# Moving a convolution kernel's input transform of the second sequence in among the first unit's products, with copies of 1008 columns

## The chip, the cores and the metric

The kernel runs on one core of one Trainium2 chip. The core's engines run side by side, each through its own queue in order: TensorE (PE in the profile, with its weight loads as PEld), VectorE (DVE), ScalarE (ACT), GpSimd (POOL) and SyncE (SP), which here only issues transfers. PE writes its results to PSUM, eight banks of 512 float32 columns for each of 128 partitions; DVE and ACT read them from there. The metric is the device time of one execution in microseconds (us), lower is better.

## What is computed

```
B, S, C = 2, 2048, 1024          # x: (B, S, C), w: (3, C, C), bfloat16
xp = pad(x, one row of zeros at both ends of S)
y = sum(einsum('bsc,cd->bsd', xp[:, k:k + S, :], w[k]) for k in range(3))
y = (y - mean) * (g / sqrt(var + 1e-5)) + b
return silu(y)
```

It is a convolution of width 3 along the sequence, over two sequences of 2048 rows with 1024 channels in and out, then a normalisation by channel and SiLU.

## The kernel before

The convolution is done in a transformed domain (Winograd's method, six output rows from eight points): each sequence is cut into NB = 342 blocks of R = 6 rows, NJ = 8 transformed values j stand for each block and channel, and for each j there is one matrix product over the channels. The stages are:

- **Input transform.** The rows of a sequence are loaded in NW = 17 row blocks ("windows") of 128 rows, 21 transform blocks each (the last one, the "short block", has 33 rows and 6). For each window and each tile of 128 channels one matmul (L265) multiplies the window by a fixed matrix `rm`, 128 x 168 columns (8 values j times 21 blocks; 48 columns in the short block). A **transform job** is a group of such matmuls into a pair of PSUM banks, followed by one copy to the tile `T_sb` in SBUF, by ACT (L276) or DVE (L278); the builder chooses the engine by a running clock of its own (`ends`, `busy`, `cost`). `T_sb` is one tile of [128, 8 channel tiles, 8 j, 684 blocks]; sequence 1 has the columns 0 to 341 of its last axis, sequence 2 the columns 342 to 683. Before the change a job is one window and four channel tiles, four matmuls and a copy of 672 columns, and a sequence has 33 jobs.
- **Weight transform.** The three weight matrices of 128 output channels become six (`u0`, `u1`, `u2`, two each) by sums on POOL (L174, L184, L194) with some scaling on ACT (L162, L180) and DVE. For the first 128 channels `prepare_first(0)` issues it, behind the job with number `W0_USE`.
- **Units.** A unit (`Unit.run`) is 128 output channels of one sequence: eight products in the order j = 1, 3, 2, 4, 5, 6, then 0 and 7 (which run behind product 5 and 6 of the following unit, `prev.rest`). A product is eight matmuls of 342 columns (L311), one for each channel tile, which accumulate in one PSUM bank. Copies by ACT (L322, L324) and sums by DVE (L329) combine them, ACT applies SiLU (L334), and the result goes out by transposing transfers (L443) and stores (L456). There are 16 units; unit 0 is sequence 1, unit 1 sequence 2 with the same weights. Unit 0 uses banks 0 to 3.

The order on every engine is that in which the builder emits the instructions (`manual_schedule`); the tile framework adds a semaphore wait wherever an instruction touches a region of a tile that an earlier instruction on another engine wrote or read. `ahead` emits jobs one after another, with the bank pairs 0, 2, 4, 6 in turn. The last `AMONG` = 18 jobs of sequence 2 are emitted by the object `between`, which `product` calls after each matmul: up to product 5 of unit 0, in the bank pairs 4, 6, 1 in turn.

The loads stand on SP's queue in this order: windows 1 to 16 and then window 0 of sequence 1, with the three weight loads of the first 128 channels behind the fifth, seventh and ninth; then the same windows of sequence 2, with the weights of the next 128 channels behind the sixth, ninth and twelfth. Window 0 has a tile of its own (`xfirst`, with a zero row, loaded in two parts of 112 and 15 rows, L124 and L125); the others share twelve buffers (`xpool`), so that a load waits for the jobs of the window twelve loads earlier. When unit 0 has been emitted, `xpool` is closed and the next weights (L146) use its space.

Of the kernel before, what the change touches and what calls it, by code (L numbers as in the profile page):

```python
# [11 lines left out]
BF16 = mybir.dt.bfloat16  # L12
# [3 lines left out]
P = 128  # L16
R = 6
NJ = 8
W0_AT = (4, 6, 8)
W0_USE = 18  # L20
W1_AT = (5, 8, 11)
AMONG = 18
XBUFS = 12
WT = 21

@with_exitstack
def kernel(
# [10 lines left out]
    nc = tc.nc  # L38
    B, S, C = x.shape
# [63 lines left out]
    rm = transform_matrix()  # L103

    clock = {"pe": 3500.0, "act": 0.0, "dve": 0.0, "dma": 2600.0}
    cost = {"act": (0.833, 190.0), "dve": (1.042, 150.0)}
    bank_free = {}

    def ends(e, size):
        return max(clock[e], clock["pe"] + 100.0) + cost[e][0] * size + cost[e][1]  # L110

    def busy(e, size):
        clock[e] = ends(e, size)

    order = list(range(1, NW)) + [0]
    xwin = {}
    xfirst = consts.tile([P, C], BF16, name="xfirst")
    nc.gpsimd.memset(xfirst[0:1, :], 0.0)

    def load_x(bi, wi):  # L120
        if wi == 0:
            xw = xfirst
            cut = (P - 1) // 16 * 16
            nc.sync.dma_start(out=xw[1:1 + cut, :], in_=x[bi, 0:cut, :])  # L124
            nc.sync.dma_start(out=xw[1 + cut:P, :], in_=x[bi, cut:P - 1, :])  # L125
        else:
            xw = xpool.tile([P, C], BF16, name="xw")
            lo = R * WT * wi - 1
            hi = min(lo + P, S)
            nc.sync.dma_start(out=xw[0:hi - lo, :], in_=x[bi, lo:hi, :])  # L130
        clock["dma"] += 730.0
        xwin[bi, wi] = xw, clock["dma"]

    w_all = w.rearrange("k (ct p) d -> p k ct d", p=P)
# [4 lines left out]
    def load_w(pair, k, half=None):  # L139

        if (pair, "tile") not in raw:
            raw[pair, "tile"] = wpools[pair % 2].tile([P, 3, CT, 2, P], BF16, name=f"wch{pair % 2}")
        wch = raw[pair, "tile"]
        h0, h1 = (0, 2) if half is None else (half, half + 1)
        cols = slice((2 * pair + h0) * P, (2 * pair + h1) * P)
        nc.sync.dma_start(  # L146
            out=wch[:, k, :, h0:h1].rearrange("p c h d -> p c (h d)"), in_=w_all[:, k, :, cols]
        )
        clock["dma"] += 1200.0 * (h1 - h0)
        for h in range(2):  # L150
            raw[2 * pair + h] = wch[:, :, :, h]
# [74 lines left out]
    ident = consts.tile([P, P], BF16, name="ident")  # L226
    make_identity(nc, ident)

    def params():

        v = ps[:, 7].bitcast(BF16)[:, 0:4 * DC]
        nc.tensor.transpose(v, rows, ident[0:4 * DC, 0:4 * DC])
        nc.scalar.copy(prm, v.rearrange("p (q dc) -> p q dc", q=4))
# [12 lines left out]

    def t_jobs(bi):

        for wi in order:
            n = LAST if wi == NW - 1 else WT  # L250
            rows = min(P, S - (R * WT * wi - 1))
            n0 = bi * NB + wi * WT
            nb = 1 if CT * NJ * n <= 512 else 2
            nct = CT if nb == 1 else CT // 2
            for c0 in range(0, CT, nct):
                yield xwin[bi, wi], rows, n, n0, c0, nct, nb

    def t_job(job, bank):
        (xw, there), rows, n, n0, c0, nct, nb = job
        clock["pe"] = max(clock["pe"], there, bank_free.get(bank, 0.0))  # L260
        size = nct * NJ * n
        src = ps[:, bank:bank + nb, 0:size // nb]
        v = src.rearrange("p b (c j n) -> p b c j n", j=NJ, n=n)
        for c in range(nct):
            nc.tensor.matmul(  # L265
                v[:, c * nb // nct, c % (nct // nb)], lhsT=xw[0:rows, (c0 + c) * P:(c0 + c + 1) * P],
                rhs=rm[0:rows, :, 0:n], start=True, stop=True,
            )
        dst = T_sb[:, c0:c0 + nct, :, n0:n0 + n].rearrange("p (b c) j n -> p b (c j) n", b=nb)
        src = src.rearrange("p b (q n) -> p b q n", n=n)  # L270
        clock["pe"] += nct * NJ * n / 2.3
        e = min(("act", "dve"), key=lambda k: ends(k, size))
        busy(e, size)
        bank_free[bank] = clock[e] + 100.0
        if e == "act":
            nc.scalar.copy(dst, src)  # L276
        else:
            nc.vector.tensor_copy(dst, src)  # L278
# [8 lines left out]
    class Unit:  # L287
# [64 lines left out]
        def rest(self, between, last=5, first=6):  # L352


            return [
                (min(last, 5), self.silu_inner), (last, lambda: self.last(between)),
                (first, lambda: self.first(between)),
            ]

        def run(self, between, also=(), prepare=None):  # L360

            def behind(n):
                for at, f in also:
                    if at == n:
                        f()

            b0, b1, b2, b3 = self.bank
            sl = slice(self.lo, self.hi)  # L370
            sd = dpool.tile([P, 2, NB], FP32, name="sd")[:, :, sl]
            t0 = dpool.tile([P, 2, NB], FP32, name="t0")[:, :, sl]
            t2 = dpool.tile([P, 2, NB], FP32, name="t2")[:, :, sl]
            self.y23 = t1 = ypool2.tile([P, 2, NB], FP32, name="t1")[:, :, sl]
            self.product(3, 1, False, between)
            pa = self.copy(3)
            behind(1)
            self.product(0, 3, False, between)
            pb = self.copy(0, by=4.0)
            behind(2)  # L380
            self.product(3, 2, True, between)
            self.copy(3, dst=sd[:, 0])
            self.combine(sd[:, 1], pa, 2.0, b3, ALU.subtract)
            behind(3)
            self.product(0, 4, True, between)
            behind(4)
            self.combine(b1, b0, -2.0, pb)
            for t, a in ((t0, -0.0125), (t1, -0.05), (t2, -0.2)):
                self.combine(t, self.low, a, sd)
            idle(dve_work)  # L390
            if prepare:
                prepare_w(prepare)
            self.product(2, 5, False, between)
            pc = self.copy(2)
            if not prev:
                for _ in range(4):
                    between()
            behind(5)
            self.product(2, 6, True, between)
            self.combine(b3, b2, -0.5, pc)  # L400
            self.combine(self.low, self.high, -1.6, t0)
            self.combine(t1, self.high, -0.4, t1)
            self.combine(self.high, self.high, -0.1, t2)
            behind(6)
            if prepare:
                idle(act_work)
                idle(dve_work)
# [61 lines left out]
    def ahead(jobs, job_n):  # L469
        for job in jobs:  # L470
            t_job(job, job_n % 4 * 2)
            if job_n == 0:
                params()
            if job_n == 4:
                scales()
            if job_n == W0_USE:
                prepare_first(0)
            job_n += 1

    jobs0 = list(t_jobs(0))  # L480
    ahead(jobs0, 0)
    for i, wi in enumerate(order):
        load_x(1, wi)
        if i in W1_AT:
            load_w(0, W1_AT.index(i), 1)
    jobs1 = list(t_jobs(1))
    ahead(jobs1[:-AMONG], len(jobs0))

    class Between:

        n = done = 0
        jobs = jobs1[-AMONG:]

        def __call__(self):
            self.n += 1
            while self.jobs and self.done * 46 < self.n * AMONG:
                t_job(self.jobs.pop(0), (4, 6, 1)[self.done % (3 if self.n <= 4 * CT else 2)])
                self.done += 1

    between = Between()  # L500
    seq = [(dc, bi) for dc in range(DC) for bi in range(B)]
# [1 line left out]
    for i, (dc, bi) in enumerate(seq[:-1]):  # L503
        unit = Unit(dc, bi, i % 2 * 4)
        unit.run(
            between, prev.rest(between, *((4, 5) if i >= len(seq) - 3 else (5, 6))) if prev else (),
            1 if i == 0 else 2 if i == 2 else dc + 2 if bi == 1 and 0 < dc < DC - 2 else None,
        )
        if i == 0:
            while between.jobs:  # L510
                between()
            xwin_scope.close()
            olast = ctx.enter_context(tc.tile_pool(name="olast", bufs=3))
            wpools[1] = ctx.enter_context(tc.tile_pool(name="wpool1", bufs=1))
        if i in (0, 4, 8):
            for k in range(3):
                load_w(i // 4 + 1, k)
        if i == len(seq) - 2:
            prev.turn(olast, ((1, R), (0, 1)))
        elif prev:  # L520
            prev.turn()
        if before:
            before.store()
        before, prev = prev, unit
# [49 lines left out]
```

## Time and profile before

| | us |
|---|---|
| median of 3 runs (lowest, highest) | 191.89 (191.7, 192.23) |
| the profiled execution | 191.58 |
| its span, first to last instruction | 189.8 |
| busy in it: PE, DVE, ACT, POOL | 177.1, 157.0, 111.3, 136.8 |
| first transform matmul | 3.89 |
| first matmul of a product | 27.04 |
| the last window of sequence 1 (`xfirst`) is there, its jobs start | 20.02 |

The span is counted from the first instruction; outside it lie 191.58 - 189.8 = 1.78 us. "Busy" of PE is from the start of a matmul to its modelled end, and matmuls overlap, so that the distance of starts says more than the busy time. In a line of the timeline stand the start, the time, engine, line, operation, written tile <- read tiles, shapes, the number of instructions, and in brackets how long the engine was idle before and what ended that. The granted clock of TensorE is 0.993 of full over the span.

### The profile page before, as it was taken

The numbers are of one execution on the slowest core, as the hardware profiler recorded it, in microseconds if no ns is written. First come the engines' busy times: TensorE is split into PE (matmuls) and PEld (weight loads), VectorE is DVE, ScalarE is ACT, GpSimd is POOL, SyncE is SP. The second block draws the span as 40 slices with busy tenths as digits, with TensorE's granted clock in tenths as the row PEclk, the third lists the DMA queues.
The fourth block names the chain that finished last, engine by engine and source line by source line (L and its number), as shares of the span: only waits on it lengthen the run. The fifth ranks groups of instructions, "written<-read, shape, count | busy, mean of one in ns | idle before, by whom it ended". The sixth has DMA issues, their size and how long they took to land.

```text
span 189.8 us, 3717 instructions
## 1 busy us (share of the span) xinstructions
PE 177.1 (93%) x1397; PEld 126.3 (67%) x1397; DVE 157.0 (83%) x222; ACT 111.3 (59%) x187; POOL 136.8 (72%) x76
## 2 busy tenths in 40 slices
PE   1978989999999999999999999999999999999990
PEld 1966758666666666666666666666666666669980
DVE  5588976689978799998799989889988996769680
ACT  3688876783547474546445654655455556454790
POOL 5559999905798869999999999889999972000000
PEclk9999999999999999999999999999999999999997
DMA  5999999075060929398659494997495696867544
GB/s 180 325 329 301 343 335 301 23 203 134 6 118 20 195 54 206 95 268 204 115 129 161 108 200 137 226 209 134 108 208 115 144 109 129 173 136 161 133 99 108
DMA packets 86832, 31.71 MB, mean 167 GB/s; under 512 B 73438, under 2 KB 82654, under 8 KB 86814
## 3 DMA queue, kind: packets, MB, share of 16 engines
q1 hardware_dynamic: 85775, 31.23, 71.8%
q10 hardware_dynamic: 1039, 0.25, 0.6%
q8 instruction: 11, 0.18, 0.4%
q14 instruction: 7, 0.06, 0.1%
HBM read 14.82 MB, written 8.39 MB: 122 GB/s over the span
## 4 chain that ended last, share of the span: by engine, by line
PE 81%; DMA 10%; ACT 3%; SPq 2%; issue 1%; DVE 1%
PE ps L311 77%; DMA xw<-in_x_dram 7%; PE ps L265 4%; DMA xfirst<-in_x_dram 3%; ACT yT L334 2%; SPq L130 2%; SPq L146 1%; PE ps L419 1%; DVE T_sb L278 0%; ACT T_sb L276 0%; ACT o L420 0%; DVE o L420 0%; ACT pc L322 0%
## 5 line engine op out<-in xcount | busy, mean ns | idle before, releaser
L311 PE MATMUL ps<-T_sb,u 128*128 128x342 bf16 (+2 forms) x816 | 120.0, 299 | 0.3
L311 PEld LDWEIGHTS <-u 128*128 128x128 bf16 x816 | 76.8, 97 | 33.6 <-issue 0.5
L194 POOL TENSOR_TENSOR u<-e,w1x 128x1024 bf16<-128x1024 f32 x32 | 70.3, 2222 | 12.3 <-DVE e L176 12.1
L311 PE MATMUL ps<-T_sb,wch 128*128 128x342 bf16 (+2 forms) x272 | 42.5, 299 | 0.0
L334 ACT ACTIVATE yT<-ps,beta,scale 128x342 bf16<-128x342 f32 (+5 forms) x51 | 34.1, 704 | 11.8 <-PE ps L311 11.8
L329 DVE SCALAR_TENSOR_TENSOR t<-ps,sd 128x684 f32<-128x684 f32 (+2 forms) x51 | 39.1, 821 | 0.6
L194 POOL TENSOR_TENSOR u<-e,wch 128x1024 bf16<-128x1024 f32 x16 | 37.6, 2370 | 1.0 <-DMA wch<-in_w_dram 0.4
L311 PEld LDWEIGHTS <-wch 128*128 128x128 bf16 x272 | 25.7, 97 | 11.5
L322 ACT COPY pc<-ps 128x342 f32<-128x342 f32 (+2 forms) x34 | 14.5, 427 | 31.9 <-PE ps L311 29.4
L265 PE MATMUL ps<-rm,xw 128*128 128x168 bf16 (+1 forms) x256 | 25.8, 247 | 6.8 <-DVE rm L100 3.9
L276 ACT CAST T_sb<-ps 128x672 bf16<-128x672 f32 (+1 forms) x37 | 25.5, 737 | 7.9 <-PE ps L265 7.8
L278 DVE CAST T_sb<-ps 128x672 bf16<-128x672 f32 x29 | 23.7, 855 | 7.4 <-PE ps L265 7.0
L265 PEld LDWEIGHTS <-xw 128*128 128x128 bf16 (+1 forms) x256 | 21.1, 104 | 11.5 <-DMA xw<-in_x_dram 5.7
L329 DVE SCALAR_TENSOR_TENSOR ps<-ps,t 128x684 f32<-128x684 f32 (+2 forms) x34 | 28.3, 831 | 0.6
L176 DVE SCALAR_TENSOR_TENSOR e<-wch 128x1024 f32<-128x1024 bf16 x14 | 27.1, 1937 | 0.0
L329 DVE SCALAR_TENSOR_TENSOR ps<-ps,pc 128x342 f32<-128x342 f32 (+2 forms) x34 | 16.9, 498 | 8.9 <-PE ps L311 7.0
L174 POOL TENSOR_TENSOR e<-wch 128x1024 f32<-128x1024 bf16 x8 | 19.0, 2372 | 3.9 <-DMA wch<-in_w_dram 3.9
L334 ACT ACTIVATE yT<-t,beta,scale 128x684 bf16<-128x684 f32 (+2 forms) x17 | 15.7, 925 | 0.0
L329 DVE SCALAR_TENSOR_TENSOR sd<-pc,ps 128x342 f32<-128x342 f32 (+2 forms) x17 | 8.3, 487 | 8.4 <-ACT sd L322 8.3
L329 DVE SCALAR_TENSOR_TENSOR t<-ps,t 128x684 f32<-128x684 f32 (+2 forms) x17 | 13.9, 817 | 0.0
L322 ACT COPY sd<-ps 128x342 f32<-128x342 f32 (+2 forms) x17 | 7.3, 429 | 10.2 <-PE ps L311 10.2
L324 ACT ACTIVATE pc<-ps 128x342 f32<-128x342 f32 (+2 forms) x17 | 7.5, 441 | 9.4 <-PE ps L311 5.9
(39 smaller groups left out, 38.0 us busy)
## 6 DMA issues: line engine op xcount, KB each, us to landing
xw<-in_x_dram SPq DMA_DIRECT2D x30, 256.0 KB
out_dram<-o SPq DMA_DIRECT2D x28, 192.0 KB
wch<-in_w_dram SPq DMA_DIRECT2D x9, 512.0 KB
out_dram<-o SPq DMA_DIRECT2D x14, 120.0 KB
wch<-in_w_dram SPq DMA_DIRECT2D x6, 256.0 KB
xfirst<-in_x_dram SPq DMA_DIRECT2D x2, 224.0 KB
out_dram<-o SPq DMA_DIRECT2D x3, 128.0 KB
out_dram<-o SPq DMA_DIRECT2D x16, 0.5 KB
```

The lines of the kernel that those rows point to most:

```text
L130: nc.sync.dma_start(out=xw[0:hi - lo, :], in_=x[bi, lo:hi, :])
L174: eng.tensor_tensor(e, w0, w2, op=ALU.add)
L176: eng.scalar_tensor_tensor(out=e, in0=f, scalar=4.0, in1=h, op0=ALU.mult, op1=ALU.add)
L194: nc.gpsimd.tensor_tensor(u[:, i], sums[dc, q], o, op=op)
L265: nc.tensor.matmul(v[:, c * nb // nct, c % (nct // nb)], lhsT=xw[0:rows, (c0 + c) * P:(c0 + c + 1) * P], rhs=rm[0:rows, :, 0:n], start=Tru ...
L276: nc.scalar.copy(dst, src)
L278: nc.vector.tensor_copy(dst, src)
L311: nc.tensor.matmul(self.bank[q], lhsT=lhsT, rhs=T_sb[:, ct, j, nsl], start=not add and ct == 0, stop=ct == CT - 1, skip_group_check=add,)
L322: nc.scalar.copy(dst, self.bank[q])
L324: nc.scalar.mul(dst, self.bank[q], by)
L329: nc.vector.scalar_tensor_tensor(out=out, in0=in0, scalar=scalar, in1=in1, op0=ALU.mult, op1=op1)
L334: nc.scalar.activation(self.yT[:, rows, self.lo:self.hi], src, ACT.Silu, bias=beta[:, dc:dc + 1], scale=scale[:, dc:dc + 1])
```

## The change

- **Jobs of two windows.** A job takes two neighbouring windows, one in each bank of its pair, and up to three channel tiles: six matmuls (two windows times three tiles) or four, and one copy of 2 x 504 = 1008 columns, or 2 x 336 = 672. A pair of windows has three jobs (3, 3 and 2 channel tiles). The short block is a job by itself, eight matmuls and 384 columns. A sequence has 25 jobs. Source and destination of a copy have the axes (window, channel tile and j, block).
- **Order of the windows.** The short block first, then windows 2 to 15, then 0 and 1. Window 0 is loaded as rows 0 to 127, without the zero row, into an ordinary buffer; its jobs use a second matrix `rm0`, which is `rm` moved up by one partition, made by one matmul and one ACT copy (`first_matrix`) behind job 0. `xfirst`, its memset and the load in two parts are gone.
- **All of sequence 2's jobs are emitted among unit 0's products.** 23 of them (`EARLY`) are spread over the 32 matmuls of products 1 to 4 in proportion to their columns, in the bank pairs 4, 6, 1 in turn; the other two stand between product 5 and product 6 (`between.rest`), in the pairs 6 and 4.
- **Loads.** The second 128 channels' weights are issued behind all windows of sequence 2, in the order 0, 2, 1.
- **Builder's constants.** `W0_USE` 18 -> 15, and larger fixed costs in the builder's clock, which choose ACT or DVE for a copy.

```diff
-    order = list(range(1, NW)) + [0]
+    order = [NW - 1] + list(range(2, NW - 1)) + [0, 1]
...
+        xw = xpool.tile([P, C], BF16, name="xw")
+        lo = max(R * WT * wi - 1, 0)
+        hi = min(lo + P, S)
+        nc.sync.dma_start(out=xw[0:hi - lo, :], in_=x[bi, lo:hi, :])
...
+    def first_matrix():
+
+        v = ps[0:P - 1, 5, 0:NJ * WT]
+        nc.tensor.matmul(v, lhsT=ident[:, 1:P], rhs=rm.rearrange("p j n -> p (j n)"), start=True, stop=True)
+        nc.scalar.copy(rm0[0:P - 1].rearrange("p j n -> p (j n)"), v)
...
-        src = ps[:, bank:bank + nb, 0:size // nb]
+        nb, size = len(wins), nct * NJ * n
+        src = ps[:, bank:bank + nb, 0:size]
         v = src.rearrange("p b (c j n) -> p b c j n", j=NJ, n=n)
...
+        for q, (xw, _, mat, rows) in enumerate(wins):
+            for c in range(nct):
+                nc.tensor.matmul(
+                    v[:, q, c], lhsT=xw[0:rows, (c0 + c) * P:(c0 + c + 1) * P], rhs=mat[0:rows, :, 0:n],
+                    start=True, stop=True,
+                )
-        dst = T_sb[:, c0:c0 + nct, :, n0:n0 + n].rearrange("p (b c) j n -> p b (c j) n", b=nb)
+        dst = T_sb[:, c0:c0 + nct, :, n0:n0 + nb * n].rearrange("p c j (b n) -> p b (c j) n", b=nb)
         src = src.rearrange("p b (q n) -> p b q n", n=n)
...
-    jobs1 = list(t_jobs(1))
-    ahead(jobs1[:-AMONG], len(jobs0))
+    for k in (0, 2, 1):
+        load_w(0, k, 1)
 
     class Between:
...
+        def do(self):
+            t_job(self.jobs[self.done], (4, 6, 1)[self.done % 3] if self.done < EARLY else (6, 4)[(self.done - EARLY) % 2])
+            self.cols += self.size[self.done]
+            self.done += 1
 
         def __call__(self):
             self.n += 1
-            while self.jobs and self.done * 46 < self.n * AMONG:
-                t_job(self.jobs.pop(0), (4, 6, 1)[self.done % (3 if self.n <= 4 * CT else 2)])
-                self.done += 1
+            while self.done < EARLY and self.cols * 4 * CT < min(self.n, 4 * CT) * sum(self.size[:EARLY]):
+                self.do()
+
+        def rest(self):
+            while self.done < len(self.jobs):
+                self.do()
```

## The prediction, made before the changed kernel was run

> **What bounds the kernel now.** I read the page, then the chain of waits in order of time, then the timeline of the stretch that the change rewrites. The chain says where a gain can come from:
>
> ```profile
> 14.18 5.79 DMA xfirst<-in_x_dram
> ...
> 20.48 5.24 DMA xw<-in_x_dram
> ...
> 27.92 0.29 PE ps L311 x2
> 28.21 0.29 PE ps L265 x4
> 28.50 0.43 PE ps L311 x3
> ...
> 40.54 136.18 PE ps L311 x952
> ```
>
> Columns: start, length, what. Until 26.5 us the transfers of x decide; then PE does, and from 40.54 on (unit 1's first product) 952 products follow without a gap, 143 ns each. That code and all behind it is unchanged, so the change is worth exactly the shift of 40.54. The four transform matmuls of a job take 0.29 us, 72 ns each. How the mixed stretch runs now:
>
> ```profile
> 28.05 0.45 PE L265 MATMUL ps<-rm,xw 128*128 128x168 bf16 x4
> ...
> 28.33 0.60 PE L311 MATMUL ps<-T_sb,u 128*128 128x342 bf16 x3
> 28.60 0.86 DVE L278 CAST T_sb<-ps 128x672 bf16<-128x672 f32 x1 [1.19 <-PE ps L265]
> ...
> 28.77 0.45 PE L265 MATMUL ps<-rm,xw 128*128 128x168 bf16 x4
> ...
> 29.06 0.45 PE L311 MATMUL ps<-T_sb,u 128*128 128x342 bf16 x2
> ...
> 29.26 0.73 ACT L276 CAST T_sb<-ps 128x672 bf16<-128x672 f32 x1 [0.54 <-PE ps L265]
> ```
>
> The job's matmuls start at 28.05 and end at 28.34; the products that follow start at once (28.33) and the copy, which starts 0.26 later on DVE (0.20 on ACT: 29.06 to 29.26), runs beside them until 29.46. **No product waits for the copy of the job in front of it**: products read sequence 1's columns of T_sb, the copies write sequence 2's. This is the cover to watch. Where PE does wait for a copy, it goes on 0.05 us behind its end (ACT's copy 35.20 + 0.77 = 35.97, PE at 36.02).
>
> **The change, part by part.**
>
> *Start of the first product.* Before 27.04. Sequence 1's windows land at the same bytes as now: xfirst at 20.02, which ends that sequence; the dip of the transfers to 237 GB/s between 16.4 and 18.6 (329 to 379 around it) could give back 0.7 us, so 19.3 to 20.0. Copies of 1008 columns do not occur. ACT's two sizes (rows below) give (0.751 - 0.494)/288 = 0.89 ns a column, so 0.751 + 336 x 0.89 ns = 1.05 us; bounds 1.02 (from the fastest, 0.72) and 1.13 (in proportion). DVE has one size here; its sums L329 go from 0.50 to 0.83 over 342 columns, 0.97 ns each, so 0.855 + 0.33 = 1.18, in proportion 1.28; I take 1.20.
>
> ```profile
> L276 ACT CAST T_sb<-ps 128x672 bf16<-128x672 f32 x35 | 24.6, 751 | 7.8 <-PE ps L265 7.8
> L278 DVE CAST T_sb<-ps 128x672 bf16<-128x672 f32 x29 | 23.7, 855 | 7.4 <-PE ps L265 7.0 <-ACT T_sb L276 0.2
> ...
> L276 ACT CAST T_sb<-ps 128x384 bf16<-128x384 f32 x2 | 1.0, 494 | 0.0
> ```
>
> ACT has to do the two weight scalings (1.06 + 1.05) behind job 15. That job's windows are there at about 14.3 (the tenth window now lands at 14.21, the eleventh some 0.7 later; less three quarters of a window, since the short block is ahead); 1.15 of matmuls and ACT's copies bring it to 16.6, the scalings to 18.7, its last copies of sequence 1 (0.75, 1.05) and the first job of the last pair (1.05) to 21.2 with 0.1 of overlap each. By the transfers alone it is 19.3 + 0.43 + 0.20 + 1.05 = 21.0. **I take 21.2** (20.9 to 22.3): 5.8 us earlier than now. u0 is ready by then (at 15.7 now, less the 0.5 by which its weights come earlier), u1 is needed near 28 and comes near 23.
>
> *PE's own work from there to unit 1.* 48 products x 0.143 = 6.86; 128 transform matmuls x 0.0725 = 9.28; the short block 0.17: **16.3 us**. Now it is 6.86 + 64 x 0.0725 + 0.16 = 11.7, and it takes 40.54 - 27.04 = 13.5, so 1.8 us are waits for banks and copies. With only such waits, say 2.1, unit 1 would start at 21.2 + 16.3 + 2.1 = 39.6.
>
> *The waits that the change adds.* The instruction list of the changed program, with the semaphores, shows what the diff does not: 18 of unit 0's product matmuls wait for a copy of sequence 2's jobs, of the last job emitted for the same channel tile. In the list of before only two do, the first of product 1 and of product 5, whose banks were a job's. The cells don't overlap; but the destination now has the axes (window, channel and j, block) out of the order of their strides, and the framework seems to treat it as the whole stretch between its ends, which goes through sequence 1's columns. The waits are in the program, whatever the reason. Their price: a product that stands directly behind its job waits 0.26 + 1.20 + 0.05 = 1.51 us for a DVE copy of 1008, 0.20 + 1.05 + 0.05 = 1.30 for an ACT copy, 1.00 for ACT's 672; PE is in order, so nothing passes. By place (p2/2 is product 2, channel tile 2, counted from 0):
>
> - directly behind a DVE copy: p1/3, p2/2, p3/2, p4/4: 4 x 1.51 = 6.0
> - directly behind an ACT copy: p1/1, p2/3, p3/4: 3 x 1.30 = 3.9; p4/6 (672 columns): 1.0; p5/0, one matmul later: 1.16
> - partly covered by a job or products in between: p1/6 0.27, p2/0 0.20, p2/6 and p3/6 0.59 each (0.26 + 0.855 + 0.05 - 0.57), p4/3 0.37, p6/3 0.55, p6/6 0.21: 2.8
> - covered: p3/0, p4/0; and 0.4 for job 1, whose banks the last copy of sequence 1 frees
>
> Sum **15.3 us**. The stage then takes 16.3 + 15.3 = 31.6, and unit 1 starts at 21.2 + 31.6 = 52.8 instead of 40.54: **+12.3 us**. The ordinary bank waits (2.1) are inside: with PE held at each copy, banks are free in time.
>
> *What costs nothing.* SP's queue: sequence 2's loads wait for buffers of windows twelve earlier, now released later, but PE now takes some 3.6 us for a pair (26.6 us for the 7.3 pairs in products 1 to 4) against 1.6 us of transfer; without that cover, at PE's bare 1.75 us a pair, a late load would cost its delay. The second weights, behind x, land near 35; POOL's sums with them (31.83 now) feed unit 2, 9 us behind unit 1's start. The following weight loads (38.34 now) wait for the last job, 2 us before unit 1 as now. The extra matmul and ACT copy for rm0 (0.2 and 0.3 us) fall where PE waits for the parameter rows anyway (until 5.16). The removed memset (0.94 on POOL) covered nothing.
>
> Sum: 189.8 + 12.3 = 202.1 span, + 1.78 = 203.9 for an execution like the profiled one, which lies 0.31 under the median: **204.2 us**.
>
> A rule that makes it worse stands in the Trainium skill, "TensorE: Matmul & The Clock Gate", section "A second HAM failure mode: psum-queue depth-cycling": a kernel that cycles through PSUM leaves PE idle briefly between groups of matmuls, and its clock then swings between half and full rate. The row here: from 11.08 to 14.21 PE runs 20 matmuls, 1.45 of 3.1 us, and at 18.07 it still does 24 in 1.68 us. By the rule the stage's 16.3 us would double, by the row they stay; I go by the row, since the new stage has about the same share (16.3 of 31.6).
>
> **The rivals.**
>
> - *The waits are there but already satisfied, so that only the bank waits count.* Unit 1 starts at 39.6, -0.9: 191.0 us, faster. For it: the matmuls of 28.33 to 29.06 above show PE going on beside the copies. Against it: those have no wait in the list. It decides from where the copy of a job ends before the product behind it is reached, and no row has a copy of 672 or more under 0.72 us, when the next matmul is due at once. To come out even at all, 12.3 of the 15.3 us would have to vanish.
> - *Half of the direct waits are hidden* (matmuls emitted earlier than I count): 12.1/2 = 6 less, 198.2 us. Against it: the order list gives the places.
> - *PE falls to half rate in the gaps.* PE's start-up shows the price: 35 matmuls between 3.9 and 9.4, about 140 ns each, against 72 later. Over the whole stage + 16.3, 220.5; over half of it 212.
> - *x of sequence 2 comes too late.* 16 windows at 0.8 us from 20.0 end at 33; PE reaches the last pair near 46. Hidden.
>
> **How the numbers follow.** The forecast has 0.83, half of the waits 0.06, half rate 0.07, the waits satisfied 0.04. The range of the forecast itself: first product 20.9 to 22.3 (-0.3, +1.1), copies at their bounds over about 9 direct waits (-0.3, +0.7), the partly covered waits gone altogether (-2.8), a tenth of half rate (+1.6): 200.8 to 207.6. What lies outside is less than 2 in 10, so it is the range. About 0.3% (0.6 us) can be told from no change: slower 0.95, within it 0.02 and faster 0.03, the waits satisfied.
>
> **What would show it.** In the new profile the products' line must have idle time in front of it, some 12 us or more in all, ended by copies of T_sb on ACT and DVE; the chain from about 21 to 53 must alternate between PE and these copies; PE's slices there must fall to about half, PE's weight loads too. The gapless run of products must still be 136 us long and start near 52.8. The first product near 21.2 and copies of 1.05 and 1.20 check the terms. Wrong would be: products without such idle time (then the first rival), transform matmuls at 140 ns (then the clock), or a wait on transfers of x after 22.

## The result, and the profile after

| | before | after |
|---|---|---|
| median, us (lowest, highest) | 191.79 (191.49, 192.23), 6 runs | 207.24 (206.02, 208.88), 6 runs |
| ratio to before, 95% interval | | 1.0793 [1.0754, 1.0831] |
| the profiled execution / its span | 191.58 / 189.8 | 207.7 / 205.9 |
| granted clock of TensorE over the span | 0.993 | 0.978 |
| first product of unit 0 starts | 27.04 | 21.11 |
| first product of unit 1 starts | 40.54 | 55.61 |
| the stage between these two | 13.50 | 34.50 |

The kernel became 15.45 us slower. The chain of waits of the changed kernel (start, length, what) shows the new stage:

```profile
9.44 5.06 DMA xw<-in_x_dram
...
17.73 4.21 DVE T_sb L284 x4
...
22.61 1.05 ACT T_sb L282
...
23.70 0.45 PE ps L317 x2
24.15 0.45 PE ps L271 x6
...
24.69 1.22 DVE T_sb L284
...
25.95 0.30 PE ps L317
...
26.94 0.84 PE ps L271 x6
...
30.24 0.45 PE ps L271 x6
...
55.32 136.47 PE ps L317 x954
```

L317 is the product now, L271 the transform matmul, L282 and L284 the copies by ACT and DVE. The transfers leave the chain at 14.50, at 25.72 before; from there it holds PE and the copies only, and from the first product on the two alternate: six matmuls, then a copy alone, then a product. Six transform matmuls take 0.45 at 24.15 and at 30.24, but 0.84 at 26.94: that is another effect, below. The run of products without a gap takes 136.47 us, of which 0.29 are unit 0's last two; before it took 136.18. Nearly all of the loss lies ahead of it: 55.61 - 40.54 = 15.07 of the 16.1 us by which the span grew. The rest is at the very end: the last copy of the output ends 8.75 us behind the last product of this run in both profiles, and the transfers behind it end 1.0 us later in this execution, which lies 0.46 above the median.

The timeline of one such alternation, the places where PE waited (in total, times, longest), and the copies by shape from 17 to 58 us, all of the changed kernel:

```profile
23.99 0.60 PE L271 MATMUL ps<-rm,xw 128*128 128x168 bf16 x6
...
24.69 1.21 DVE L284 CAST T_sb<-ps 128x1008 bf16<-128x1008 f32 x1 [2.29 <-PE ps L271]
...
25.95 0.30 PE L317 MATMUL ps<-T_sb,u 128*128 128x342 bf16 x1 [1.37 <-DVE T_sb L284]
```

```profile
PE ps L317 <- DVE T_sb L284: 6.5, 7, 1.4
...
PE ps L317 <- ACT T_sb L282: 5.5, 6, 1.1
```

```profile
L284 DVE CAST T_sb<-ps 128x1008 bf16<-128x1008 f32 x11 | 13.0, 1205 | 8.3 <-PE ps L271 7.3 <-ACT sd L328 1.0
L282 ACT CAST T_sb<-ps 128x1008 bf16<-128x1008 f32 x11 | 11.3, 1044 | 9.2 <-PE ps L271 9.2
```

The copy ends at 25.90, the product starts at 25.95: it waited for it, although it reads other columns. In the profile before, the same place had the product at 28.33 beside the copy of 28.60. Thirteen such waits make 12.0 us of idle PE.

PE's busy time in stretches shows the other effect. In the traces of all ten kernels the changes of the granted clock lie whole multiples of 3.41 us apart (here at 26.30, 29.71, 50.19 and 53.61), so the stretches are cut there. Columns: stretch, length, PE's busy time and count of matmuls, then the granted clock, the share of the DMA engines and GB/s.

```profile
22.89:26.30 3.41, 1.23 (x12) 1.00 0.94 347
26.30:29.71 3.41, 3.41 (x23) 0.50 0.51 165
29.71:33.13 3.42, 1.70 (x19) 1.00 0.63 187
33.13:36.54 3.41, 2.20 (x23) 1.00 1.02 201
36.54:39.95 3.41, 1.90 (x21) 1.00 0.00 1
39.95:43.37 3.42, 2.00 (x21) 1.00 0.00 0
43.37:46.78 3.41, 1.96 (x21) 1.00 0.00 0
46.78:50.19 3.41, 1.63 (x14) 1.00 0.01 2
50.19:53.61 3.42, 3.33 (x16) 0.50 0.00 0
```

PE's clock was half of full in two stretches, 6.8 us together. Each of them follows a stretch in which PE was busy for less than half of the time (1.23 and 1.63 of 3.41); behind 1.70 and more the clock stayed full. A PE that is 3.41 of 3.41 "busy" at clock 0.50 is only slow.

### The profile page after: what moved, and what is told of

Same layout as the page of the kernel before. It is cut to its first block, busy times and chain, and to the rows that moved or that the text cites. A ratio compares the mean times of both kernels' runs of the same rounds, so it can differ in the third digit from the quotient of the medians.

```text
span 205.9 us, 3711 instructions
## 1 busy us (share of the span) xinstructions
PE 180.5 (88%) x1398; PEld 128.5 (62%) x1398; DVE 156.4 (76%) x213; ACT 112.2 (54%) x181; POOL 135.0 (66%) x75
## 4 chain that ended last, share of the span: by engine, by line
PE 77%; DVE 6%; ACT 6%; SPq 4%; DMA 2%; issue 1%; DVEq 0%
PE ps L317 71%; DVE T_sb L284 6%; PE ps L271 6%; ACT T_sb L282 3%; SPq L121 3%; DMA xw<-in_x_dram 2%; ACT yT L340 2%; SPq L137 1%; PE ps L422 1%; ACT o L423 0%; ACT sd L328 0%; DVE o L423 0%; DVEq L284 0%; ACT pc L328 0%
## 5 line engine op out<-in xcount | busy, mean ns | idle before, releaser
L317 PE MATMUL ps<-T_sb,u 128*128 128x342 bf16 (+2 forms) x816 | 123.1, 302 | 12.2 <-DVE T_sb L284 6.5
L317 PEld LDWEIGHTS <-u 128*128 128x128 bf16 x816 | 77.6, 98 | 41.6 <-issue 8.0
L185 POOL TENSOR_TENSOR u<-e,w1x 128x1024 bf16<-128x1024 f32 x32 | 70.3, 2224 | 23.9 <-DVE e L167 23.7
L317 PE MATMUL ps<-T_sb,wch 128*128 128x342 bf16 (+2 forms) x272 | 42.5, 299 | 0.0
L284 DVE CAST T_sb<-ps 128x1008 bf16<-128x1008 f32 (+2 forms) x20 | 21.9, 1121 | 21.2 <-PE ps L271 20.1
L185 POOL TENSOR_TENSOR u<-e,wch 128x1024 bf16<-128x1024 f32 x16 | 36.6, 2308 | 1.0 <-DMA wch<-in_w_dram 0.4
L282 ACT CAST T_sb<-ps 128x1008 bf16<-128x1008 f32 (+2 forms) x30 | 25.7, 899 | 17.3 <-PE ps L271 17.3
L271 PEld LDWEIGHTS <-xw 128*128 128x128 bf16 (+2 forms) x272 | 23.8, 108 | 16.5 <-issue 8.7
L271 PE MATMUL ps<-rm,xw 128*128 128x168 bf16 (+2 forms) x272 | 28.4, 254 | 6.2 <-DVE rm L99 3.3
L317 PEld LDWEIGHTS <-wch 128*128 128x128 bf16 x272 | 25.7, 97 | 11.5
L167 DVE SCALAR_TENSOR_TENSOR e<-wch 128x1024 f32<-128x1024 bf16 x14 | 29.3, 2092 | 0.0
```

The source lines that it names most:

```text
L167: eng.scalar_tensor_tensor(out=e, in0=f, scalar=4.0, in1=h, op0=ALU.mult, op1=ALU.add)
L185: nc.gpsimd.tensor_tensor(u[:, i], sums[dc, q], o, op=op)
L271: nc.tensor.matmul(v[:, q, c], lhsT=xw[0:rows, (c0 + c) * P:(c0 + c + 1) * P], rhs=mat[0:rows, :, 0:n], start=True, stop=True,)
L317: nc.tensor.matmul(self.bank[q], lhsT=lhsT, rhs=T_sb[:, ct, j, nsl], start=not add and ct == 0, stop=ct == CT - 1, skip_group_check=add,)
```

## The experiments

Each kernel computes the whole reference. The diffs are against the changed kernel, unless they say otherwise; times are medians of runs beside runs of the kernel before (191.99 for the first four, 192.05 for the last four), and the intervals are those of the ratio to it.

The sequence's rows do not land at the same time in each execution: the 76th matmul on a window of x, which waits for a transfer in all of these kernels, starts at 14.55 in the changed kernel's profile and between 14.28 and 15.46 in the others. The first product and unit 1 move with it. So the length of a stage, or the time counted from this matmul (called "from the landing" below), says more than the start.

### One tile of T_sb for each sequence (e3_tiles)

```diff
-    T_sb = tpool.tile([P, CT, NJ, NT], BF16, name="T_sb")
+    T_sb = [tpool.tile([P, CT, NJ, NB], BF16, name=f"T_sb{q}") for q in range(B)]
```

(and both uses index it by the sequence). A copy of sequence 2 then can't touch what a product of sequence 1 reads. Matmuls, copies and loads stay the same.

> The changed kernel with T_sb as two tiles, one for each sequence: the same copies and matmuls in the same order, but the instruction list has no wait of unit 0's products for copies of sequence 2 any more. Theory (the added waits are the whole loss): unit 1's first product starts near 39.6 us and the time is about 191.0 us, at or just under the kernel before (191.8), with TensorE's clock at full rate in the stage. Rival (copies of 1008 columns through three pairs of banks are too slow whatever waits there are): the stage stays over 25 us long and the time above 200. Rival (the clock falls to half rate because of the mixture itself): the waits vanish but some 2.6 us remain, 193 to 194 us.

Measured: **190.38 us** (190.0 to 190.65), ratio 0.9905 [0.9872, 0.9938]. No product waits for a copy any more; unit 1 starts at 39.66, the stage is 18.05. So the waits, with what they bring along, made all of the loss (the kernel with one copy for each window, below, says so too), and without them the change is a gain. What is left in its chain are two waits of another kind:

```profile
23.39 0.45 PE ps L271 x6
...
23.93 1.22 DVE T_sb L284
...
25.19 0.59 PE ps L271 x6
...
33.44 1.22 DVE T_sb L284
...
34.70 0.60 PE ps L271 x6
```

Here a transform matmul, not a product, waits for a copy: its bank pair is still being read.

### One copy for each window, T_sb in one tile (e4_split)

```diff
-        if e == "act":
-            nc.scalar.copy(dst, src)
-        else:
-            nc.vector.tensor_copy(dst, src)
+        for q in range(nb):
+            if e == "act":
+                nc.scalar.copy(dst[:, q], src[:, q])
+            else:
+                nc.vector.tensor_copy(dst[:, q], src[:, q])
```

> The changed kernel with one copy instruction for each window of a job (504 or 336 columns, two behind each other) instead of one for both; one T_sb tile as before. The instruction list has no wait of unit 0's products for copies of sequence 2. Theory (the waits come from both windows in one copy, and are the loss): about as the run with two tiles, plus what a second instruction costs where a bank is waited for, 0.1 to 0.2 us a copy, so 191 to 193 us. Rival (the waits are not the loss): above 200 us.

Measured: **189.2 us** (188.7 to 189.51), ratio 0.9845 [0.9798, 0.9891]. The waits are gone with this too, though the two sequences share a tile; and it is 1.2 us better than the two tiles, where the expectation, 191 to 193, had it a little worse. Its chain from 1.1 us behind the first product on:

```profile
22.73 0.38 PE ps L271 x3
23.11 0.29 PE ps L318 x2
23.40 0.44 PE ps L271 x6
```

It goes on like this, PE behind PE: none of the 1.22 us waits for a bank of the kernel with two tiles is in it. The copies of 504 columns took 0.676 us each on DVE (x23) and 0.615 on ACT (x22), so that two cost more than one of 1008 (1.35 against 1.205, 1.23 against 1.044); but the first starts behind the first window's matmuls and its bank is done earlier. The stage is 38.62 - 21.65 = 16.97 us.

### Copies for each window only in the first twelve of sequence 2's jobs (e5_half)

```diff
-            t_job(self.jobs[self.done], ...)
+            t_job(self.jobs[self.done], ..., self.done < 12)
```

(the last argument says whether the copy is made window by window.) This leaves half of the waits: those of products 1 and 2 and of product 3's first matmul go.

> The changed kernel, with one copy for each window only in the first twelve of sequence 2's jobs: the waits of products 1 and 2 and of product 3's first are gone, those from product 3 on stay. Theory (the loss is the sum of the single waits): by the prediction's terms 1.30 + 1.51 + 0.27 + 0.20 + 1.51 + 1.30 + 0.59 = 6.7 us less, less some half a microsecond of bank waits that come back, and about one half-rate stretch of the clock less (1 us): 199.5 to 202 us. Rival (one wait brings the rest, and taking half away moves the loss to the other half): less than 3 us off, above 204.

Measured: **200.42 us** (199.89 to 200.56), ratio 1.0426 [1.0378, 1.0474], 6.8 less than the changed kernel. Product 3 starts at 28.35 (36.38 in the changed kernel). The total is as expected, but with luck: the start of product 3 gained 8.0 us, and 1.8 us were lost again behind it (product 3 to unit 1 takes 21.03 us, 19.23 in the changed kernel), where the clock is worse. These stretches from product to product show it (start of products 1, 3, 4, 5, unit 1; columns: PE's busy time, clock, share of the DMA engines, GB/s):

```profile
20.96:28.35 7.39, 7.15 (x85) 1.00 1.05 387
28.35:36.17 7.82, 5.33 (x43) 0.78 0.62 126
36.17:43.46 7.29, 3.69 (x36) 0.94 0.01 2
43.46:49.38 5.92, 5.92 (x27) 0.50 0.09 27
```

PE is 97% busy at full clock where no product waits. The stretches between the changes of the clock, from where the waits return (columns as before):

```profile
28.96:32.37 3.41, 1.45 (x15) 1.00 1.17 220
32.37:35.79 3.42, 2.89 (x17) 0.50 0.06 9
35.79:39.20 3.41, 2.44 (x26) 1.00 0.02 5
39.20:42.61 3.41, 1.63 (x14) 1.00 0.00 0
42.61:46.03 3.42, 2.57 (x11) 0.50 0.00 0
46.03:49.44 3.41, 3.41 (x19) 0.50 0.17 52
```

Three stretches, 10.2 us, are at half rate, more than the 6.8 of the changed kernel, where the expectation had less. Again a stretch less than half busy stands ahead of each fall (1.45 and 1.63 of 3.41).

### Idle places filled with matmuls that add nothing (e6_busy)

```diff
+                if between.n in (1, 3, 10, 11, 18, 20, 28, 30) and not prev:
+                    for _ in range(14):
+                        nc.tensor.matmul(
+                            self.bank[q][:, 0:NJ * WT], lhsT=zero, rhs=rm.rearrange("p j n -> p (j n)"),
+                            start=False, stop=False, skip_group_check=True,
+                        )
```

`zero` is a tile of zeros; at eight of the places with a wait PE does 14 matmuls that add zero to the product's bank, 112 in all, about 1.0 us at each. All waits stay.

> The changed kernel with 14 matmuls of 168 columns (1.0 us at full rate) behind the jobs at eight places where a product waits directly for a copy; they multiply by zeros and add into the product's own bank, so they change no result and take up time that PE waits anyway. All waits stay. Theory (2.8 us of the loss beyond the predicted 12.3 is the clock at half rate in two stretches of 3.4 us, which the idle time brings on): the clock stays at full rate in the stage and the time falls by 2 to 3 us, to 204 to 205. Rival (the extra is in the waits themselves, each longer than counted): the time stays at 207 or rises by what the matmuls take.

Measured: **204.2 us** (203.83 to 204.67), ratio 1.0629 [1.0579, 1.0679]: 112 matmuls more and 3.0 us less. The same stretches (products 1, 2, 3, 4, 5, unit 1), first of this kernel, then of the changed one without filling:

```profile
20.91:28.13 7.22, 6.34 (x73) 1.00 0.85 302
28.13:35.01 6.88, 5.99 (x69) 1.00 0.94 230
35.01:41.89 6.88, 5.99 (x70) 1.00 0.05 7
41.89:48.93 7.04, 5.57 (x66) 1.00 0.01 3
48.93:52.74 3.81, 3.37 (x26) 1.00 0.07 20
```

```profile
21.11:29.27 8.16, 5.42 (x44) 0.82 0.84 298
29.27:36.38 7.11, 4.19 (x41) 0.97 0.79 186
36.38:43.27 6.89, 3.96 (x43) 1.00 0.00 1
43.27:50.28 7.01, 3.69 (x38) 0.99 0.00 1
50.28:55.61 5.33, 4.97 (x26) 0.69 0.04 11
```

With PE 79 to 88% busy the clock is 1.00 throughout; unit 1 starts at 52.74 instead of 55.61, and the stage is 31.83 instead of 34.50, 2.7 us shorter. In the first and the last stretch of the changed kernel, which hold its two half-rate stretches, most of the difference lies: 8.16 - 7.22 = 0.94 and 5.33 - 3.81 = 1.52.

### What the rest of the change is worth, on the kernel with copies for each window

Three edits on top of `e4_split`, and one on top of the third. The second weights back among sequence 2's windows, as before:

```diff
-    for wi in order:
+    for i, wi in enumerate(order):
...
-    for k in (0, 2, 1):
-        load_w(0, k, 1)
+        if i in (5, 8, 11):
+            load_w(0, (5, 8, 11).index(i), 1)
```

> The run with one copy for each window (189.2 us), with the second 128 channels' weights put back among sequence 2's windows, behind the sixth, ninth and twelfth, as in the kernel before. Theory (that part of the change costs and brings nothing, since PE reaches the last windows of sequence 2 late enough): within 0.3 us of 189.2. Rival (the place of the weights matters): three loads of about 1.1 us each in front of the last windows, PE waits for x in products 3 and 4, 1 to 3 us more, 190 to 192.

Measured: 189.53 us (189.3 to 190.53), ratio 0.9869 [0.9818, 0.9919]; the intervals overlap, so no difference can be told. Unit 1 starts at 38.86 instead of 38.62. The profile shows more than the medians: PE waits 0.7 us for transfers of x in product 3 (until 29.41 and 31.80), which it does nowhere behind the first product in `e4_split`, and the stage is 18.08 against 16.97. In this execution x landed 0.87 us earlier (14.28 against 15.15), which hides it in the start of unit 1.

Seven of sequence 2's jobs ahead of unit 0 again (`EARLY` 16):

```diff
-EARLY = 23
+EARLY = 16
...
+    jobs1 = list(t_jobs(1))
+    ahead(jobs1[:7], 25)
...
-        jobs = list(t_jobs(1))
+        jobs = jobs1[7:]
```

> The run with one copy for each window (189.2 us), with the first seven jobs of sequence 2 (the short block and two pairs of windows) emitted ahead of unit 0 and not among its products. Theory (the gain of the change, once the waits are gone, is that products start while sequence 2 is still being loaded): the first product starts some 3 us later, near 24.5, the stage behind it is shorter by 32 x 0.0725 + 0.17 = 2.5 us, and what the copies hold PE back is on the path again: 189.5 to 190.5 us. Rival (it does not matter where PE does its transform matmuls): 189.2 within 0.3.

Measured: 190.91 us (190.51 to 191.76), ratio 0.9937 [0.991, 0.9963], 1.7 us more than without it; a little more than expected. The first product starts at 25.87, 4.2 later (0.3 of it from the landing), and the stage is shorter by 2.6 (14.40 against 16.97). Moving these seven behind the first product, as the change does, is thus worth something by itself.

The first unit's two weight scalings from ACT to POOL:

```diff
-        double_w(dc, nc.scalar)
-        for q, eng in ((1, nc.scalar), (2, nc.gpsimd)):
-            even_part(dc, q, nc.gpsimd, eng)
-            transform_w(dc, q)
+        even_part(dc, 1, nc.gpsimd, nc.gpsimd)
+        double_w(dc, nc.gpsimd)
+        transform_w(dc, 1)
+        even_part(dc, 2, nc.gpsimd, nc.gpsimd)
+        transform_w(dc, 2)
```

> The run with one copy for each window (189.2 us), with the two weight scalings of the first channels (ACT, 16.84 to 18.85) moved to POOL, and the builder's choice of engine for the copies following from it. Theory (before the first product ACT's and DVE's copies decide, not the transfers, which end near 18): ACT gains 2.1 us, shared by both engines that is about 1 us, the first product starts near 20.6 and the time is 188 to 188.5, if u1 from POOL is there by product 2 (near 24.5; I count 23.8). Rival (u1 comes too late, since POOL now has 2.1 us more in front of it): PE waits at product 2 and the gain is lost, 189 to 190.

Measured: **188.27 us** (187.95 to 188.86), ratio 0.9797 [0.9751, 0.9843], the lowest median of all; its interval overlaps that of `e4_split`, though, and the slowest of its four runs (188.86) lies above the fastest there (188.7), so a gain is likely and its size open. The first product starts at 20.26 and unit 1 at 37.35, 1.4 and 1.3 us earlier than in `e4_split`, but half of that is the landing (14.46 against 15.15): from the landing to the first product it is 5.80 against 6.50, to unit 1 22.89 against 23.47. The move itself is worth 0.7 and 0.6. The timeline of POOL shows what it cost there (start, time, line, operation, written <- read):

```profile
17.49 1.04 POOL L174 TENSOR_SCALAR w1x<-wch 128x1024 bf16<-128x1024 bf16 x1
18.62 2.13 POOL L175 TENSOR_TENSOR e<-w1x,wch 128x1024 f32<-128x1024 bf16 x1
20.71 1.04 POOL L156 TENSOR_SCALAR w1x<-wch 128x1024 bf16<-128x1024 bf16 x1
21.84 4.23 POOL L185 TENSOR_TENSOR u<-e,w1x 128x1024 bf16<-128x1024 f32 x2
```

The two scalings take 1.04 each on POOL (1.06 on ACT); POOL ends the two halves of `u1`, which product 2 (from 24.28 on) and product 4 (from 31.24 on) read, at about 23.9 and at 26.07; PE has no wait for POOL.

The same with sequence 1's jobs back at one copy for both windows; no product runs beside those (the diff is against the kernel with the scalings on POOL):

```diff
-        for q in range(nb):
-            if e == "act":
-                nc.scalar.copy(dst[:, q], src[:, q])
-            else:
-                nc.vector.tensor_copy(dst[:, q], src[:, q])
+        copy = nc.scalar.copy if e == "act" else nc.vector.tensor_copy
+        if n0 >= NB:
+            for q in range(nb):
+                copy(dst[:, q], src[:, q])
+        else:
+            copy(dst, src)
```

> As the run with the scalings on POOL, but sequence 1's jobs have one copy for both windows again (sequence 2's keep one for each window, so no product waits for them). Theory (a second instruction costs what lies between 0.60 x 2 and 1.04 us on ACT, some 0.15 us a copy, where the copies decide): the first product up to 0.5 us earlier than in that run and the time 0 to 0.5 us lower. Rival (copies by halves start earlier and free the banks earlier, which outweighs it): the same or up to 0.5 us higher.

Measured: 188.59 us (188.18 to 189.67), ratio 0.9819 [0.9767, 0.9871]. First product 20.95, unit 1 at 37.63, which is 5.96 and 22.64 from the landing, against 5.80 and 22.89; the intervals overlap, so nothing can be told between the two.

## Why the prediction was right, and where it was not

By its own steps:

- **Start of the first product: 21.2, measured 21.11.** The copies were sized well: 1.05 on ACT and 1.20 on DVE, measured 1.044 and 1.205. That the start agrees to a tenth is luck: in the other kernels with the same copies up to there (`e3_tiles`, `e5_half`, `e6_busy`) it lies between 20.91 and 21.61, as x lands. The two routes to the number were not equally good. By the transfers it gave 21.0, but in the changed kernel they are not in the chain after 14.50; the route over ACT's scalings holds, since moving those to POOL took 0.7 us off the time from the landing to the first product, in the kernel with one copy for each window.
- **PE's own work, 16.3.** With the waits gone and banks released by halves the stage is 16.97, and 16.67 in `e10_pool_one`, where PE has no idle time in it, so the term was some 0.4 too small; with only bank waits 18.05, where the prediction had 16.3 + 2.1 = 18.4. Its first rival, the waits satisfied, was priced at 191.0; the kernel that takes them away by two tiles takes 190.38.
- **The waits, 15.3.** The idle places stand where the list put them: products 1/1, 1/3, 2/2, 2/3, 3/2, 3/4, 4/4, 4/6, 5/0 each wait out most of a copy: 1.12 behind ACT (0.98 at 5/0, one matmul later) and 1.37 or 1.30 behind DVE for 1008 columns, 0.83 for ACT's 672 at 4/6 (from the modelled end of the matmul before; the prediction counted from the distance of starts, 0.15 more). Of the partly covered ones, 2/6, 3/6, 4/3 and 6/3 measure 0.44, 0.44, 0.21 and 0.32, where the list had 0.59, 0.59, 0.37 and 0.55; 1/6 and 2/0 do not wait. With the clock kept full the stage is 31.83 where the prediction had 16.3 + 15.3 = 31.6, unit 1 starts at 52.74 (52.8), and the time is 204.2, the predicted one. That it agrees to the tenth is luck too: PE's own work is some 0.4 longer and the waits some tenths shorter.
- **The term that was mis-sized: PE's clock.** The prediction weighed the row of 20 matmuls in 3.1 us, "by the row they stay", and kept half rate as "a tenth, +1.6" in the range and as a rival over half of the stage or all of it. Measured: 6.8 of 34.5 us at half rate, a fifth, and 34.50 - 31.83 = 2.7 us. This, 0.2 in the start of the first product and some tenths in the last transfers, is what separates 207.24 from 204.2, and what puts the median only 0.4 us below the upper end of the range; three of the six executions lie above it. The row was no counter-example. Counted back in steps of 3.413 us from 187.06, where the clock falls at the end of the profile before, its 20 matmuls lie in two stretches, from 9.57 and from 12.98, in which PE is busy for 3.02 and 2.46 of 3.41 us, far more than half. The Trainium skill, "TensorE: Matmul & The Clock Gate", section "A second HAM failure mode: psum-queue depth-cycling", says that short idle times between groups of matmuls make the clock swing between half and full; the runs agree (0.82 and 0.69 in two stretches, 1.00 in all when they are filled). The section gives no size; that the whole stage would double was the prediction's own reading, and the runs show a fifth of it at half rate.
- **The reason offered for the waits fell.** The prediction put them down to "the axes (window, channel and j, block) out of the order of their strides". Instruction lists of variants that were built and not run say otherwise: with the axes in the order of the strides the same 18 waits are there; with one, two or three channel tiles a copy and both windows in it they are there; with axes out of order in the kernel before there are none. With one copy for each window they vanish, and `e4_split` shows it on the chip. So it is the two windows in one destination that bring them; why the framework finds an overlap there stays open. The forecast didn't hang on it, because the waits were read from the instructions.
- **What costs nothing.** PE waits for no transfer of x after 22 in the changed kernel. POOL does wait 3.9 us for the second weights (its line 165), as they stand behind x; the products after 55.32 have no gap, so it is hidden. Putting the weights back, in `e7_weights`, made no difference that can be told in the time; it brought 0.7 us of waits for x.

What became of the gain: the first product comes 27.04 - 21.11 = 5.9 us earlier. The 64 transform matmuls that moved behind it take back 64 x 0.0725 = 4.6. That leaves 1.3. `e3_tiles` shows 0.9 of it (unit 1 at 39.66; its x landed 0.5 later), and `e4_split` betters it (1.9). The waits and the clock make the stage of the changed kernel 34.50 - 18.05 = 16.45 us longer than that of `e3_tiles`.

## What to carry to other kernels

Where work on one part of a tile is moved in among readers of another part, read the waits in the built instructions, at each reader: a diff shows none, and here 18 of them turned a gain of 1% into a loss of 8%. Two smaller copies, each with a plain region, can beat one larger copy that does the same columns in less time, since readers and banks come free earlier. Price a stage in which PE idles half of the time with some of it at half clock, look at PE's busy share between the clock's changes and not at the mean of the stage, and test for it by filling the idle places with work that changes nothing.

## What the runs showed of the hardware

- The clock changed only at whole multiples of 3.41 us from one another, in all ten traces; two such stretches were at half rate in the changed kernel, and three where half of the waits were left. The Trainium skill, "TensorE: Matmul & The Clock Gate", section "What's actually happening", states that the gate judges windows of about 3.4 us that run freely; the lengths here agree.
- The longest wait of PE in this stage was 1.4 us, and the clock fell all the same. The same page's section "HAM oscillation — how this bites in real kernels" gives as the rule to have no idle gap over some 3.4 us; by that none of this stage would have been slow, and the measurement decides against it: the share of busy time in a stretch counts. Of the full-rate stretches in the ten traces, from the first record of the clock (8 to 11 us) up to unit 1, those with PE busy for 1.23, 1.45, 1.63 and 1.63 of 3.41 us were followed by half rate, and all others, from 1.70 up, by full rate, so the border here lies near half. At half rate, where a matmul takes longer, 2.57 of 3.41 did not bring the full clock back and 2.89 did. Busy time is not quite what is judged: at the end of `e4_split`, where the kernel runs out, the clock fell behind a stretch with 1.89.
- The clock of the changed kernel differed from run to run, 0.964 to 0.988, and its time with it, 208.88 to 206.02; the kernels that keep PE busy had 0.991 to 0.998 in their profiles.
